# A planned kernel gets new landing times, new GpSimd costs and newly fitted offsets

## The chip, the cores and the metric

The kernel runs on one core of a Trainium2 chip. It is one program of some 108,000 instructions on TensorE (PE), VectorE (DVE), ScalarE (ACT), GpSimd (POOL) and SyncE (SP, which only issues DMAs). The metric is the device time of one execution in microseconds (us).

## The reference

Three stages follow each other on 24576 rows of 256 numbers (8 batches of 3072 rows). All data are float32.

```python
# 1. attention without softmax, z: 64 columns
attn = np.maximum(np.matmul(z, z.transpose(0, 2, 1)) / S, 0.0) ** 2
x = (u * np.matmul(attn, v)).reshape(B * S, D)
# 2. one of 8 experts for each row whose skip score is positive (hidden width 1024)
h = np.maximum(xc[mask] @ w1[e], 0.0)
y[mask] = gate_w[mask, None] * (h @ w2[e])
out[do_compute] = xc + y
# 3. a dense layer with a rational function (hidden width 2048)
h = x @ w_in
P = a[0] + a[1] * h + a[2] * h2 + a[3] * h3
Q = 1.0 + np.abs(b[0]) * np.abs(h) + np.abs(b[1]) * h2
return (P / (Q + 1e-06)) @ w_out
```

## The kernel before

Every float32 operand of a large product is kept as two parts, a rounded one and the rest (names with h and l: `ah`/`al`, `mgh`/`mgl`, the two halves of V, W and mx), and each product is three matmuls.

**Attention** is cut into 1152 ticks. A tick makes 128x512 scores S (L683, L684, 0.467 in the planner's numbers) in a PSUM bank, ScalarE applies Relu (L687), Square (L690) and copies the result to `ah` (L428; sometimes VectorE does, L430), VectorE writes `al` (L698), and PE multiplies both with V (L706). Twelve ticks make a row of 256 outputs; the last one is followed by L766 (`xs`, the product with u, which empties the accumulator), by transposes of `xs` (L782) and by the routing, a chain of small operations (numbered r0 to r24) that ends in indirect DMAs from GpSimd's queue.

**Experts** are units of 256 rows by 256 hidden columns: first layer h (L1133), `mgh` by ScalarE (L1326), `mgl` by VectorE (L1329), second layer (L1152). There are seven groups of 32. For six of them PE runs little else meanwhile. I call these stretches the expert stages; they are those with a high DMA rate. The weights W of each unit (1 MB) are loaded anew for each.

**The dense layer** has 768 units: h (L1144), then a chain on three engines: `mu` = |h| and `mp` by ScalarE (L1334, L1335), q0 = `mq` (L1341 on GpSimd or VectorE, L1339 on ScalarE), q1 and later `gl` by L424 (on either VectorE or GpSimd), logarithm and exponential by ScalarE, and L1347, L1348, L1361, L1362, L1364 on VectorE, then the second layer (L1162). 616 of these units are interleaved with attention ticks. The last 152, at the end of the program, have no attention beside them and use a slightly different chain (L1351 to L1357).

**What sets the order.** Nothing is scheduled by hand. `Flow.add` collects some 14,000 steps, each with a wished time, the steps it comes after, the ring buffers it takes and frees, and a text of costs. `Flow.run` places them one after the other in a model of the queues, and the order in which it places them is the order of the program on each engine. In a cost text such as `"G1.038 Q2.9 L3.3"` a letter is an engine (P TensorE, A ScalarE, D VectorE, G GpSimd, Q the DMA queue), the number is how long the step holds it, a bar separates alternatives of which the planner picks one, and `L` adds time that holds no engine before the result counts as there. Behind an engine's last cost comes `LAT` (2.0 for Q). A final `s` marks a VectorE step and a final `t` a GpSimd step that exclude each other: an `s` step is put off while a `t` step runs, and any GpSimd step while an `s` or `t` step of VectorE runs. The wished time of a step is its place in a regular pattern plus an offset from `PAR`, one for each kind of step and kind of stretch (S, t, a for attention; m, n, x, y for units; `.s` is the program's start). Rings are buffers taken in turn: 5 PSUM banks `b` for scores, h and transposes, 2 `ah`, 2 `al`, 3 each of `mu`, `mq`, `mgh`, `mgl`, 4 `wr` for raw loads of z and V, 8 W, 12 V.

`spacers` are unused columns put ahead of the first tile of a name, which shift the SBUF addresses of what is allocated after it.

## Time and profile before

| | |
|---|---|
| Median of 3 runs | 5405.6 us (5404.68 to 5406.18) |
| The profiled execution, its own time | 5410.29 us |
| its span, first to last instruction | 5408.6 us |
| TensorE busy | 5245.5 us (97%) |
| VectorE busy | 4504.9 us (83%) |
| ScalarE busy | 4193.2 us (78%) |
| GpSimd busy | 3326.9 us (62%) |
| mean granted TensorE clock | 0.997 |

A busy time is the union of an engine's instructions. TensorE's matmuls overlap each other and their ends are modelled, so the pace of a run of matmuls is read from many in a row. In a row of waits stand the engine and line that stood idle, what ended the wait, and then us in total, how many times, and the longest. In a row of the timeline the numbers are start and duration in us; a bracket at the end is the idle time of the engine just before it and what ended it. In a row of groups, the count is followed by busy us, mean ns of one, and the idle time before them with what ended it.

### The profile page before, as it was taken

The page shows a single profiled execution, that of the slowest core. Times are in us where ns is not written, and L with a number is a line of the kernel's source. Part 1 is how long each engine was busy: PE and PEld are TensorE (multiplying, and loading weights), DVE is VectorE, ACT ScalarE, POOL GpSimd, SP SyncE. Part 2 cuts the span into 40 slices and gives each one's busy share as a digit, 9 for nine tenths or more (in the row PEclk, how much of TensorE's full clock was granted, in tenths as well). Part 3 has the DMA queues.
Part 4 walks back from the last instruction along what each step waited for, and adds up shares of the span by engine and source line. Part 5 has one row for each costly group of instructions (what it writes and reads, how often), then busy time and mean ns, then how long its engine had stood idle before and what let it go on. Part 6 is the DMA issues. An engine that isn't in the chain of part 4 may idle for free.

```text
span 5408.6 us, 107807 instructions
## 1 busy us (share of the span) xinstructions
PE 5245.5 (97%) x39885; PEld 4985.3 (92%) x39885; DVE 4504.9 (83%) x7338; ACT 4193.2 (78%) x7643; POOL 3326.9 (62%) x4822
## 2 busy tenths in 40 slices
PE   8999999999999999999999999999999999999988
PEld 8999999999999999899999998999989998889777
DVE  6774789857999958999949999859999589987999
ACT  8885788857888857788848787758888578876998
POOL 5863466635656646557636566536576466666998
PEclk9999999999999999999999999999999999999999
DMA  6747311064100173000372001361011630035000
GB/s 214 251 146 293 105 53 34 30 244 147 52 26 28 56 282 105 24 25 29 106 268 68 27 29 53 137 233 44 25 51 45 242 114 23 28 115 192 22 16 14
DMA packets 218093, 540.19 MB, mean 100 GB/s; under 512 B 30607, under 2 KB 129534, under 8 KB 180946
## 3 DMA queue, kind: packets, MB, share of 16 engines
q1 hardware_dynamic: 188754, 448.71, 23.7%
q0 software_dynamic: 28800, 84.48, 4.5%
q8 instruction: 316, 5.18, 0.4%
q14 instruction: 223, 1.83, 0.1%
HBM read 413.38 MB, written 149.01 MB: 104 GB/s over the span
## 4 chain that ended last, share of the span: by engine, by line
PE 61%; DVE 20%; ACT 6%; POOL 5%; issue 5%; DMA 1%; SPq 0%; DVEq 0%; POOLq 0%; ACTq 0%
PE accA L706 20%; PE h L1144 11%; PE accM L1162 10%; PE h L1133 6%; PE accM L1152 5%; PE S L683 3%; PE S L684 3%; DVE mq L1362 3%; DVE mp L1347 2%; DVE mgh L1361 2%; DVE al L698 2%; DVE h L1348 2%; DVE mq L424 2%; DVE mq L1364 2%; POOL mq L424 1%
## 5 line engine op out<-in xcount | busy, mean ns | idle before, releaser
L706 PE MATMUL accA<-V,ah 128*128 128x256 f32 x9216 | 1271.2, 281 | 21.5 <-ACT ah L428 11.7
L1144 PE MATMUL h<-mx,W 128*128 128x512 f32 x4608 | 1212.8, 399 | 42.0 <-DVE mgl L1357 28.0
L706 PEld LDWEIGHTS accA<-V,ah 128*128 128x128 f32 x9216 | 1161.7, 189 | 36.8 <-ACT ah L428 16.5
L1144 PEld LDWEIGHTS h<-mx,W 128*128 128x128 f32 x4608 | 816.1, 189 | 193.7 <-DVE mgl L1357 37.1
L698 DVE TENSOR_TENSOR al<-S,ah 128x512 fp32r<-128x512 f32 x1152 | 785.1, 683 | 199.6 <-ACT ah L428 185.4
L424 POOL TENSOR_TENSOR mgl<-mq,mu 128x512 fp32r<-128x512 f32 x486 | 641.1, 1319 | 380.4 <-DVE mq L1364 244.5
L1162 PE MATMUL accM<-W,mgh 128*128 128x256 f32 x6144 | 841.6, 280 | 8.3 <-ACT mo L1225 5.9
L687 ACT ACTIVATE S<-S 128x512 f32<-128x512 f32 x1152 | 677.1, 590 | 174.8 <-PE S L684 163.8
L1162 PEld LDWEIGHTS accM<-W,mgh 128*128 128x128 f32 x6144 | 776.0, 189 | 16.5 <-ACT mo L1225 7.5
L1341 POOL TENSOR_SCALAR mq<-mu,coef 128x512 f32<-128x512 f32 x584 | 489.7, 839 | 490.1 <-ACT mu L1334 486.6
L706 PE MATMUL accA<-V,al 128*128 128x256 f32 x4608 | 734.0, 282 | 19.9 <-DVE al L698 19.0
L690 ACT ACTIVATE S<-S 128x512 f32<-128x512 f32 x1152 | 671.4, 585 | 25.5
L706 PEld LDWEIGHTS accA<-V,al 128*128 128x128 f32 x4608 | 623.8, 189 | 32.6 <-DVE al L698 27.3
L1334 ACT ACTIVATE mu<-h 128x512 f32<-128x512 f32 x768 | 455.8, 593 | 237.2 <-PE h L1144 221.7
L424 POOL TENSOR_TENSOR mq<-mq,mu 128x512 f32<-128x512 f32 x458 | 606.5, 1326 | 41.6 <-DVE mq L1341 11.3
L1347 DVE TENSOR_TENSOR mp<-mp,h 128x512 f32<-128x512 f32 x768 | 520.7, 679 | 105.2 <-ACT mp L1335 100.0
L428 ACT ACTIVATE ah<-S 128x512 fp32r<-128x512 f32 x958 | 573.2, 598 | 39.3 <-PE accA L706 11.0
L1335 ACT ACTIVATE mp<-h,coef 128x512 f32<-128x512 f32 x768 | 595.1, 775 | 3.0 <-DVE h L1348 2.8
L684 PE MATMUL S<-T,T 128*128 128x256 f32 x2304 | 589.8, 280 | 1.0 <-ACT T L627 0.9
L1348 DVE SCALAR_TENSOR_TENSOR h<-mp,coef,h 128x512 f32<-128x512 f32 x768 | 572.6, 746 | 4.3
L1362 DVE SCALAR_TENSOR_TENSOR mq<-mq,mgh 128x512 f32<-128x512 f32 x616 | 515.1, 836 | 20.5 <-DVE mgh L1361 0.5
L1359 ACT ACTIVATE mu<-mq 128x512 f32<-128x512 f32 x616 | 388.2, 630 | 179.6 <-DVE mq L424 100.8
(271 smaller groups left out, 9828.3 us busy)
## 6 DMA issues: line engine op xcount, KB each, us to landing
W<-wsc SPq DMA_DIRECT2D x184, 1024.0 KB, 6.8
W<-wsc POOLq DMA_DIRECT2D x48, 1024.0 KB, 5.3
Wv<-wsc SPq DMA_DIRECT2D x64, 512.0 KB, 5.4
xs<-in_u_dram SPq DMA_DIRECT2D x96, 256.0 KB, 3.2
vr<-in_v_dram SPq DMA_DIRECT2D x96, 256.0 KB, 3.1
x<-xs SPq DMA_DIRECT2D x96, 256.0 KB, 2.1
wsc<-wp SPq DMA_DIRECT2D x24, 1024.0 KB, 4.8
mr<-x SPq DMA_DIRECT2D x96, 256.0 KB, 3.4
```

The lines of the kernel that those rows point to most:

```text
L424: (nc.vector if e == "D" else nc.gpsimd).tensor_tensor(*a, **k)
L684: mm(o, lhsT=lw, rhs=T4[b, ic], start=False, stop=(jj == 1), skip_group_check=True)
L687: act(st["s"], st["s"], AF.Relu, scale=1.0 / S)
L690: act(st["s"], st["s"], AF.Square)
L698: ttt(st["lo"], st["s"], st["hi"].bitcast(F32), op=ALU.subtract)
L706: mm(accs[b, ic][:, it * TT : (it + 1) * TT], lhsT=a[:, jj * TT + it * P : jj * TT + (it + 1) * P], rhs=VV[b, jp][:, vi, jj * D : (jj + 1) ...
L1144: mm(h, lhsT=lw, rhs=rw, start=(k == 0 and i == 0), stop=(k == NK - 1 and i == 2), skip_group_check=True)
L1162: mm(accs_[it // 2][:, it % 2 * TT : (it % 2 + 1) * TT], lhsT=(gh, gl)[part][:, it * P : (it + 1) * P], rhs=w[i][:, 512 + ff * D : 512 + ( ...
L1335: pt("p1", "A.664", ["l1b"], lambda: act(buf("mp"), s["h"], AF.Identity, scale=a3, bias=a2), ["mp"])
L1347: pt("p2", "D.602", ["p1", "abs"], lambda: ttt(s["p"], s["p"], s["h"], op=ALU.mult))
L1348: pt("p3", "D.663", ["p2", "abs"], lambda: stt(s["h"], s["p"], a1, s["h"], op0=ALU.add, op1=ALU.mult), (), ["mp"])
L1362: pt("v", "D.602s", ["gh"], lambda: stt(s["q"], s["q"], CQ, s["gh"].bitcast(F32), op0=ALU.add, op1=ALU.mult))
```

## The change

Four things change; the formulas, the steps and the rings do not.

Every load and store gets an `L` with its landing time, or a larger one. Two GpSimd operations that had no mark get a `t`: the copies of 128x512 (`G.588`) and q0 (`G.78`). The load of dense weights by GpSimd's queue costs it 0.52 and not 1.038. All offsets of `PAR` have new values, and with them the order of the whole program. The spacers are three others.

```diff
-    "S.a": 10.7, "S.t": -2.83, "T1.a": -193.43, ... "T1ld.s": -299.17, ... "Vld.s": -133.16, ... "wpld.w": 4.47,
+    "S.a": 11.86, "S.t": -2.87, "T1.a": -92.99, ... "T1ld.s": -330.92, ... "Vld.s": -43.77, ... "wpld.w": -48.08,
...
-    spacers = {"T4": 16, "ah": 16, "W": 112, "mgh": 16}
+    spacers = {"T4": 16, "V": 16, "W": 48}
...
-        add(X(y), k + ("ld",), "Q.36", load, takes=[("wr", k + ("r",)), ("wr", k)])
+        add(X(y), k + ("ld",), "Q.36 L2.8", load, takes=[("wr", k + ("r",)), ("wr", k)])
...
-        add(X(y), k + ("ld",), "Q.73", load, takes=[("wr", k)])
-        add(X(yh), k + ("hi",), "G.588|A.52|D.335s", hi, after=[k + ("ld",)], takes=[("V", k)])
+        add(X(y), k + ("ld",), "Q.73 L2.5", load, takes=[("wr", k)])
+        add(X(yh), k + ("hi",), "G.588t|A.52|D.335s", hi, after=[k + ("ld",)], takes=[("V", k)])
...
-        add(xx, ("u", row), "Q.73", load, takes=[("xs", row)])
+        add(xx, ("u", row), "Q.73 L2.5", load, takes=[("xs", row)])
...
-            (18, 18, "G1.038 L2.4", lambda: r16(2), (16,), [], [], []),
-            (19, 19, "G1.038 L2.4", lambda: r16(3), (16, 17, 18, 21), [], [], [("xs", row)]),
+            (18, 18, "G1.038 L4", lambda: r16(2), (16,), [], [], []),
+            (19, 19, "G1.038 L4", lambda: r16(3), (16, 17, 18, 21), [], [], [("xs", row)]),
...
-            w_first[n][0] - 24.0, ("W", n), "Q1.46 Q1.46" if v else "Q2.9", load, after=dep,
+            w_first[n][0] - 24.0, ("W", n), "Q1.46 Q1.46 L2.2" if v else "Q2.9 L3.3", load, after=dep,
...
-        add(xx, ("W", n), "G1.038 Q2.9", load, after=[("wsc", fp)], takes=[("W", n)])
+        add(xx, ("W", n), "G.52 Q2.9 L.5", load, after=[("wsc", fp)], takes=[("W", n)])
...
-        add(y - 12.0, k + ("ld",), "Q.73 L1.6", load, after=dep, takes=[("mr", (mi, h))])
+        add(y - 12.0, k + ("ld",), "Q.73 L4.9" if m.kind == 1 else "Q.73 L2.6", load, after=dep, takes=[("mr", (mi, h))])
...
-                xe + 2.6, k + ("p1",), "G1.038 L3.4", lambda: scatter(1), after=[k + ("s0",)],
+                xe + 2.6, k + ("p1",), "G1.038 L5", lambda: scatter(1), after=[k + ("s0",)],
...
-            pt("q0", "G.78|A.707|D.46s", ["abs"], q0, ["mq"])
+            pt("q0", "G.78t|A.707|D.46s", ["abs"], q0, ["mq"])
```

The expert weights' first loads and the stores of split weights (`Wl`, `wsc1`, `wsc`) and the stores of results get an `L` in the same way.

Three places in the order of the program show what the offsets do. The numbers in the names count objects (the first) and tiles (the last); `h752` is the first layer of unit 752.

TensorE, an interleaved stretch near the end, from the last score matmul of tick 1099 on. Before:

```order
L684 MATMUL S1099_63513<-T4_7_7_62829,T1_7_3_56503 128x256
L1144 MATMUL h752_63523<-mx83_62894,W232_61272 128x512 x6
L706 MATMUL accA7_7_63093<-V7_6_56951,ah1098_63527 128x256 x8
L706 MATMUL accA7_7_63093<-V7_6_56951,al1098_63534 128x256 x4
L1162 MATMUL accM82_0_62705<-W238_62057,mgh749_63462 128x256 x4
```

and with the change:

```order
L684 MATMUL S1099_63446<-T4_7_7_62821,T1_7_3_56524 128x256
L1144 MATMUL h751_63454<-mx82_62207,W239_62144 128x512 x6
L1162 MATMUL accM82_0_62746<-W237_61873,mgh747_63285 128x256 x4
L1162 MATMUL accM82_1_62747<-W237_61873,mgh747_63285 128x256 x4
L1162 MATMUL accM82_0_62746<-W237_61873,mgl747_63406 128x256 x2
L1162 MATMUL accM82_1_62747<-W237_61873,mgl747_63406 128x256 x2
L706 MATMUL accA7_7_63100<-V7_5_57075,ah1097_63401 128x256 x8
L706 MATMUL accA7_7_63100<-V7_5_57075,al1097_63411 128x256 x4
```

Behind the scores of tick 1099 the next `ah` and `al` products were those of tick 1098; now they are those of tick 1097.

TensorE, inside an expert stage, units 276 to 278. Before:

```order
L1133 MATMUL h276_29342<-mx33_29305,W100_29029 128x256 x12
L1152 MATMUL accM32_0_29215<-W99_28976,mgh275_29310 128x256 x8
L1133 MATMUL h277_29372<-mx33_29305,W101_29109 128x256 x12
L1152 MATMUL accM32_0_29215<-W99_28976,mgl275_29319 128x256 x4
L1152 MATMUL accM33_0_29393<-W100_29029,mgh276_29366 128x256 x8
L1133 MATMUL h278_29410<-mx33_29305,W102_29181 128x256 x12
L1152 MATMUL accM33_0_29393<-W100_29029,mgl276_29370 128x256 x4
```

and with the change:

```order
L1133 MATMUL h276_29333<-mx33_29136,W100_29005 128x256 x6
L1152 MATMUL accM32_0_29196<-W99_28967,mgh275_29319 128x256 x8
L1133 MATMUL h276_29333<-mx33_29136,W100_29005 128x256 x6
L1152 MATMUL accM32_0_29196<-W99_28967,mgl275_29341 128x256 x4
L1133 MATMUL h277_29374<-mx33_29136,W101_29062 128x256 x6
L1152 MATMUL accM33_0_29384<-W100_29005,mgh276_29372 128x256 x8
L1133 MATMUL h277_29374<-mx33_29136,W101_29062 128x256 x6
L1152 MATMUL accM33_0_29384<-W100_29005,mgl276_29393 128x256 x4
```

Between h276 and the product with `mgh276` stood 24 matmuls of 256 columns; now 10 stand there, since each first layer is cut in two halves with a second layer between them.

SP, the start, from the first load of z on. Before:

```order
L589 DMA zr0_0_124<-in_z_dram 128x256
L589 DMA zr0_1_127<-in_z_dram 128x256
L665 DMA xs0_130<-in_u_dram 128x2x256
L665 DMA xs1_132<-in_u_dram 128x2x256
L1412 DMA xs_71<-dflt_117 16x2064
L639 DMA vr0_0_139<-in_v_dram 128x512
```

With the change the first four rows are the same, then come `wr1_8mu` and:

```order
L383 DMA wr1_8mq_135<-in_moe_w2_dram 128x2x256
L379 DMA wr1_9mu_138<-in_moe_w1_dram 128x2x256
L383 DMA wr1_9mq_139<-in_moe_w2_dram 128x2x256
L1412 DMA xs_71<-dflt_117 16x2064
L379 DMA wr1_10mu_146<-in_moe_w1_dram 128x2x256
L383 DMA wr1_10mq_147<-in_moe_w2_dram 128x2x256
L589 DMA zr0_2_166<-in_z_dram 128x256
L589 DMA zr0_3_176<-in_z_dram 128x256
L1412 DMA xs_71<-dflt_117 16x2064
L1396 DMA ov_73<-ovf_200 1x2
L1412 DMA xs_71<-dflt_117 16x2064 x2
L639 DMA vr0_0_240<-in_v_dram 128x512
```

The first chunk of V, `vr0_0`, was the sixth load from there on and is now the eighteenth. In the same stretch ScalarE's order is Relu of ticks 0 to 3, Square and `ah` of tick 0, Square of tick 1, and only then the copy that reads `zr0_2`; that copy stood behind the Relu of tick 0 before.

## Rows read from the trace of the kernel before

**Rows 1.** The page, first part: busy us, share of the span, instructions.

```profile
PE 5245.5 (97%) x39885; PEld 4985.3 (92%) x39885; DVE 4504.9 (83%) x7338; ACT 4193.2 (78%) x7643; POOL 3326.9 (62%) x4822
```

**Rows 2.** Windows of 135 us: bounds, length, each engine's busy us, clock, DMA.

```profile
1890.00:2025.00 135.00, 131.42 (x1106) 129.41 (x1105) 73.56 (x131) 71.57 (x134) 56.91 (x105) 1.00 0.76 279
...
5130.00:5265.00 135.00, 121.47 (x737) 107.11 (x736) 131.45 (x205) 125.09 (x213) 126.16 (x114) 0.96 0.06 20
...
sum 5400.00, PE 5245.49 PEld 4985.31 DVE 4504.91 ACT 4193.23 POOL 3326.88; mean PE 131.14 PEld 124.63 DVE 112.62 ACT 104.83 POOL 83.17
```

**Rows 3.** Waits of PE: us in total, times, longest.

```profile
PE h L1144 <- DVE mgl L1357: 28.0, 27, 3.2
PE accA L706 <- DVE al L698: 19.0, 27, 2.8
PE tp L605 <- DVE zh L598: 16.7, 6, 10.5
PE accM L1162 <- DVE mgl L1357: 13.1, 12, 2.3
PE accA L706 <- ACT ah L428: 11.7, 18, 1.5
...
PE accA L706 <- DVE xs L766: 7.0, 9, 1.7
...
PE xp L782 <- DVE xs L766: 5.7, 9, 1.5
```

**Rows 4.** Timeline around 4511 us, three engines.

```profile
4503.88 1.28 POOL L424 TENSOR_TENSOR mq<-mq,mu 128x512 f32<-128x512 f32 x1
...
4504.15 1.60 DVE L1362 SCALAR_TENSOR_TENSOR mq<-mq,mgh 128x512 f32<-128x512 f32 x1
...
4510.37 0.68 DVE L698 TENSOR_TENSOR al<-S,ah 128x512 fp32r<-128x512 f32 x1
...
4511.11 0.74 PE L706 MATMUL accA<-V,al 128*128 128x256 f32 x4 [1.38 <-DVE al L698]
```

**Rows 5.** Chain that ended last, one piece: start, us, what.

```profile
147.53 2.83 PE accA L706 x24
```

**Rows 6.** Groups by line: count, busy us, mean ns, idle before.

```profile
L698 DVE TENSOR_TENSOR al<-S,ah 128x512 fp32r<-128x512 f32 x1152 | 785.1, 683 | 199.6 <-ACT ah L428 185.4 <-PE accA L706 3.3 <-PE S L684 3.2
...
L1341 POOL TENSOR_SCALAR mq<-mu,coef 128x512 f32<-128x512 f32 x584 | 489.7, 839 | 490.1 <-ACT mu L1334 486.6 <-DVE al L698 1.3
...
L1362 DVE SCALAR_TENSOR_TENSOR mq<-mq,mgh 128x512 f32<-128x512 f32 x616 | 515.1, 836 | 20.5 <-DVE mgh L1361 0.5 <-POOL rin L760 0.5
...
L424 DVE TENSOR_TENSOR mq<-mq,mu 128x512 f32<-128x512 f32 x310 | 279.2, 901 | 3.3 <-POOL mq L1341 3.1
...
L1152 PE MATMUL accM<-W,mgh 128*128 128x256 f32 x1536 | 210.9, 280 | 0.0
```

**Rows 7.** DMA issues: count, KB each, median us from issue to landing.

```profile
vr<-in_v_dram SPq DMA_DIRECT2D x96, 256.0 KB, 3.1
...
mr<-xs SPq DMA_DIRECT2D x56, 258.0 KB, 6.3
```

**Rows 8.** Waits of all engines, one row.

```profile
POOL mti L1211 <- DMA mr<-xs: 79.3, 20, 8.3
```

**Rows 9.** Timeline of the start, four engines.

```profile
10.43 0.35 SPq L639 DMA_DIRECT2D vr<-in_v_dram  x1
...
14.02 0.62 POOL L432 TENSOR_SCALAR V<-vr 128x512 fp32r<-128x512 f32 x1 [7.23 <-DMA vr<-in_v_dram]
...
17.71 0.60 ACT L428 ACTIVATE ah<-S 128x512 fp32r<-128x512 f32 x1
...
18.45 1.83 PE L706 MATMUL accA<-V,ah 128*128 128x256 f32 x7 [1.48 <-ACT ah L428]
```

**Rows 10.** Timeline in an expert stage, one unit's first layer and `mgh`.

```profile
2009.19 1.53 PE L1133 MATMUL h<-mx,W 128*128 128x256 f32 x12
...
2010.76 0.60 ACT L1326 ACTIVATE mgh<-h 128x512 fp32r<-128x512 f32 x1 [2.55 <-PE h L1133]
```

More of the change, by code (lines that the diff above doesn't have):

```diff
@@ L1008, in plan_w1 @@
         room = [("l1a", max(0, w_last[n - NW] - 2))] if n >= NW else []
-        add(xx - 5.0, ("Wl", n), "Q.73 Q.73", load, after=room, takes=tr)
-        add(xx, ("Wh", n, 0), "A.52|D.335s|G.588", lambda e: hi(e, 0), after=[("Wl", n)], takes=[("W", n)])
-        add(xx + 0.6, ("Wh", n, 1), "A.52|D.335s|G.588", lambda e: hi(e, 1), after=[("Wh", n, 0)])
+        add(xx - 5.0, ("Wl", n), "Q.73 Q.73 L4.2", load, after=room, takes=tr)
+        add(xx, ("Wh", n, 0), "A.52|D.335s|G.588t", lambda e: hi(e, 0), after=[("Wl", n)], takes=[("W", n)])
+        add(xx + 0.6, ("Wh", n, 1), "A.52|D.335s|G.588t", lambda e: hi(e, 1), after=[("Wh", n, 0)])
         add(xx + 0.8, ("Wo", n), "D.602s|G1.245t", lambda e: lo(e, 0), after=[("Wh", n, 0)], frees=tr[:1])
         add(xx + 1.4, ("W", n), "D.602s|G1.245t", lambda e: lo(e, 1), after=[("Wh", n, 1), ("Wo", n)], frees=tr[1:])
-        add(xx + 2.0, ("wsc1", c), "Q2.9", store, after=[("W", n)])
+        add(xx + 2.0, ("wsc1", c), "Q2.9 L1", store, after=[("W", n)])
     def plan_w1prep(c, y):
@@ L1036, in store @@
             nc.sync.dma_start(out=wsc1[c].bitcast(F32), in_=st["w"].bitcast(F32))
-        add(X(y), k + ("ld",), "Q.73 Q.73", load, takes=tr)
+        add(X(y), k + ("ld",), "Q.73 Q.73 L2.7", load, takes=tr)
         for half in range(2):
             h = k + (half,)
-            add(X(y + 2.0 + 0.3 * half), h, "G.588|D.335s", lambda e, half=half: hi(e, half), after=[k + (("ld",) if half == 0 else (0,))], takes=[] if half else [("mx", k)])
+            add(X(y + 2.0 + 0.3 * half), h, "G.588t|D.335s", lambda e, half=half: hi(e, half), after=[k + (("ld",) if half == 0 else (0,))], takes=[] if half else [("mx", k)])
             add(X(y + 2.4 + 0.6 * half), h + ("l",), "G1.245t", lambda e="G", half=half: lo(e, half), after=[h], frees=tr[half : half + 1])
-        add(X(y + 4.0), ("wsc1", c), "Q2.9", store, after=[k + (0, "l"), k + (1, "l")], frees=[("mx", k)])
+        add(X(y + 4.0), ("wsc1", c), "Q2.9 L1", store, after=[k + (0, "l"), k + (1, "l")], frees=[("mx", k)])
     def whole(n):
@@ L1107, in plan_w2prep @@
         k = ("wsc", fp)
-        add(X(y), k + (0,), "Q1.46 Q1.46", load, after=[("wsc", fp - 1)] if fp else [], takes=[("W", k + ("a",)), ("W", k + ("b",))])
+        add(X(y), k + (0,), "Q1.46 Q1.46 L3", load, after=[("wsc", fp - 1)] if fp else [], takes=[("W", k + ("a",)), ("W", k + ("b",))])
         for half in range(2):
@@ L1122, in plan_w2prep @@
             add(X(y), h + ("l",), "D.602s", lambda half=half: lo(half), after=[h + ("h",)], frees=[("wr", h)])
[L1123 removed]
+        add(X(y + 0.7), k, "G1.038 Q2.9 L1", store, after=[k + (1, "l")], frees=[("W", k + ("w",))])
     def mm_l1(h, w, xh, xl, ffs=(0, 1)):
@@ L1272, in plan_half @@
         else:
-            add(xe + 1.0, k + ("p1",), "Q.73", store, after=[k + ("p0",)], frees=[("mo", (mi, h))])
+            add(xe + 1.0, k + ("p1",), "Q.73 L1.5", store, after=[k + ("p0",)], frees=[("mo", (mi, h))])
     def WV(n):
```

25 lines of the change are left out of this document (12 added, 13 removed), and 38 rows, old and new, of the table PAR.

## The prediction

> **What bounds the kernel now.** I read the page's first part, then the table of windows, then the waits of PE, and only then single stretches. TensorE is busy for 5245.5 of 5408.6 us [rows 1]; the 40 windows leave it 154.5 us idle [rows 2]. So nothing that the change does to another engine is worth more than those idle times, and the matmuls themselves are the same 39885 in another order. The windows say where the idle time sits. In the window of the expert stage PE loses 3.6 us of 135. In the last stage it loses 13.5 us, and there VectorE is busy for 131.5 of 135 us: VectorE sets the end of that stage, whatever order PE has. The waits of PE [rows 3] name what ended its idle times: `mgl` (28.0 and 13.1 us, nearly all in the last stage), `al` and `ah` of the attention ticks (19.0 and 11.7), `xs` at the ends of attention rows (7.0 and 5.7), and `zh` (16.7, of which 10.5 is the start of the program). Nothing on this list is a DMA: a late landing reaches PE only through an engine that stands behind it.
>
> Why a tick waits is seen at 4511 us [rows 4]: PE stands 1.38 us for `al`. VectorE was late because L1362, which takes 0.68 us when nothing interferes, took 1.60 us: GpSimd was in a whole-tile product until 4505.16, and L1362 ended 0.59 us after that. Everything behind it on VectorE came later by as much. PE's order left little room: from the scores of that tick to their use it had 7.0 us of other work. I count such room throughout as the matmuls that stand between in PE's order, at 0.118 us per 256 columns (24 in 2.83 us [rows 5]).
>
> **Part 1: PE's places for the attention ticks.** The new numbers draw the uses of `ah` and `al` back. Between a tick's scores and its `al` product PE has 10.8 us of other work in the median where it had 8.8; before its `ah` product 9.4 where it had 7.0. Ticks with under 7 us ahead of `al` fall from 336 to 70 of 1152. The tick of 4511 us goes from 7.0 to 13.0. The waits for `al` and `ah` are 19.0 + 11.7 = 30.7 us [rows 3]. If they go with the number of short ticks, 70/336 = 0.21 of them stay, 6.4 us, and 24 us go. If they stay whole, since `ah` has two buffers and the room from the last use of tick n-2 to the `ah` product of tick n is 5.5 us where it was 5.1, nothing goes. The row of 4511 us is nearer to the first end: `al` was late there by VectorE's queue, not by a missing buffer. I take **-16 us**, range -24 to 0. What is late next is the S bank (five in the ring): its room stays at 8.3 us, before 8.4, so I add nothing for that.
>
> **Part 2: ends of attention rows.** The first `ah` product of a row waits for L766 to empty the accumulator. From row 17 on, 24 of 79 row ends had less than 1.5 us of PE work there; now 7 have. Of 7.0 us [rows 3], 17/24 is 5. The transposes of `xs` (5.7 us) have a median of 1.4 us ahead of them where they had 1.9, so nothing is gained on them. I take **-4**, range -5 to 0.
>
> **Part 3: what the planner knows of GpSimd, and who does what.** L1362 and L424 on VectorE read two SBUF tiles. L698, of the same size but with one operand in PSUM, means 0.683 us; L1362 means 0.836 (616 times) and L424 0.901 (310 times) [rows 6]. The excess is 616 x 0.153 + 310 x 0.218 = 162 us of VectorE. It comes from GpSimd's whole-tile operations; the planner already held VectorE back for its products, and not for L1341, which ran 584 times for 489.7 us. A third of the excess, 54 us, is the most I give to L1341. VectorE also gets 25 instructions fewer (39 `ah` go to ScalarE, 21 q0 leave VectorE; V, q1 and gl come back), 25 x 0.68 = 17 us, and ScalarE 50 more, 30 us, which its 78% hide [rows 1]. Of 54 + 17 us on an engine with 83% only the stretches count in which PE waits for VectorE; I take **-6**, range -15 to 0. A reason against more: the row of 4511 us also shows the products, which the planner did know, blocking L1362. [...]
>
> **Part 4: landing times.** The planner took 0.73 + 2.0 = 2.73 us for a load of `vr`; the trace says 3.1, so it came late as a rule. It takes 5.23 now. For `mr` out of `xs` it took 4.33 against 6.3, and takes 7.63 now [rows 7]. GpSimd lost 79.3 us to late `mr` [rows 8], in a stage where it has slack: its 62% hide that. On PE's path I find only the `zh` waits outside the start, 16.7 - 10.5 = 6.2 us. I take **-3**, range -6 to 0. A longer assumed landing also holds ring buffers longer in the plan; that is priced in the next part, where it bites.
>
> **Part 5: the start.** SP's queue is moved as a whole: six loads of `wr1_8` to `wr1_10` and two more `z` chunks go ahead of the first `vr`. That has two consequences. SP needs about 0.5 us for each issue. And `vr0_0` is now the ninth taker of the four `wr` buffers and waits for `zr0_2` to be read by VectorE, whose ScalarE step stands behind the scores' first steps: ScalarE writes `ah` of tick 0 from 17.71 us [rows 9]; its steps start some 0.5 us apart, one more stands ahead of `zh0_2`, so that starts at 18.7, and VectorE is done with it near 19.8. Before, `vr0_0` went out at 10.43 and GpSimd had it at 14.02, 3.6 us later; then 0.62 us on GpSimd and about 0.68 on VectorE for the two halves. So the first product stands at 19.9 + 3.6 + 1.3 = 24.8 us, where it stood at 18.45. PE does 0.9 us of later work ahead of it. The loss is up to 5.4 us; V chunks follow at the pace of the ring, so I expect little of it back. **+5**, range 0 to +8. ScalarE, GpSimd and SP have nothing else urgent queued there.
>
> **Part 6: the expert stage.** Here the change takes room away. In 192 units (six stages of 32) PE had a median 3.3 us of work between h and the `mgh` product, and 5.6 us to the `mgl` product; now 1.2 and 2.8. ScalarE writes `mgh` in 0.60 us, starting 0.04 us after the matmuls' end in the row [rows 10]; counted from PE's next free slot this is about 0.85 us, so 0.3 us of slack is left. Queued on ScalarE between two `mgh` stand `mx`, and now and then a copy of V, which waits for a landing. Before, PE had next to nothing to wait for there, so no gain is possible. Bounds: 0, and 192 x 0.2 = 38 us if a unit waits 0.2 us on average. I take **+3**, nearer to the first: some twenty units of before had 0.9 us of room too, and the group of all 1536 `mgh` products shows 0.0 us of idle time ahead of them [rows 6]. `W` slots come free some 2.8 us sooner, which helps the loads of that stage.
>
> **Part 7: no price.** The last stage is VectorE's. Its three windows leave VectorE 3.5 us idle in the one shown, about 9 in all, so it can gain 9 at the most; I take 0, range -9 to +6. The spacers keep what a matmul reads together 64 bytes apart (modulo 128), as before; I take 0 for them.
>
> **The sum.** -16 - 4 - 6 - 3 + 5 + 3 = -21 us. The profiled run took 5410.3 us, 4.7 above the median of 5405.6; 5389 against the first is 5385 against the second. **Forecast: 5385 us.**
>
> **The rivals.**
> First, **slower: the expert stage has no slack left.** If ScalarE reaches `mgh` late, by a V copy that waits for its load or by an `mx`, each unit's wait falls straight on PE. At 0.2 us per unit it costs 38 us instead of 3: 5385 + 35 = 5420. It outweighs the gains from (21 + 3)/192 = 0.125 us per unit on. For it: the room fell by more than half in the stage with the most DMA. Against: ScalarE is busy only 71.6 of 135 us there [rows 2]. Chance 0.24, with all other ways to lose as much.
> Second, **no change: room is not what ticks lack.** The buffers of `ah` and VectorE's queue, both as full as before, set the waits; parts 1 and 3 come to 0 and the time is 5385 + 16 + 6 = 5407. This is also the case in which new landing times change numbers of a plan and not the chip. Chance 0.21.
> Third, **the block only changes hands**: kept off VectorE's back, L1341 waits for VectorE instead (it means 0.84 us now [rows 6]) and what follows on GpSimd comes later; part 3 is 0, the time 5391. Chance 0.15.
> The forecast itself has 0.40.
>
> **How the numbers follow.** A measurement of this kernel tells about 0.2%, 11 us, from no change: 5395 and 5416 are the edges. The forecast and the third rival are faster (0.55), the second the same (0.21), the first slower (0.24). The terms' own ends give 5405.6 - 24 - 5 - 15 - 6 - 9 = 5347 below; above, the slower rival at 5420 must be half inside. Range 5350 to 5424.
>
> **What would show it right or wrong.** Part 1: waits of PE for `al` and `ah` near 15 us in sum, not 31. Part 3: L1362 near 0.80 us in the mean. Part 4: the wait of GpSimd for `mr` well under 79 us. Part 5: the first accA matmul at 23 to 25 us. Part 6: in the windows of the expert stages PE as busy as before (131 to 135 us) and no wait of PE for `mgh`; a row "PE accM <- ACT mgh L1326" of 20 us or more means the first rival. If PE's idle total falls and the time does not, the count of room was the wrong measure.

## The result, and the profile after

The changed kernel takes 5465.9 us in the median of four runs (5455.98 to 5466.58) where the kernel before took 5405.9 beside it: ratio 1.0105, 95% interval 1.0088 to 1.0123. It is slower by 60 us by the medians, 57 by the ratio; 5385 was forecast, and 5424 was the upper end of the range. The profiled execution of after is its fastest run, 5455.98 us with a span of 5454.3; it is compared with the span of 5408.6 before, so the two profiles hold 45.7 us of the difference.

The first part of the page of after, beside [rows 1]:

```profile
PE 5296.4 (97%) x39885; PEld 5020.7 (92%) x39885; DVE 4508.2 (83%) x7313; ACT 4198.2 (77%) x7693; POOL 3282.6 (60%) x4797
```

PE's idle time is 5454.3 - 5296.4 = 157.9 us, before 163.1. So PE's idle time did not grow: PE is **busy** 50.9 us longer, with the same 39885 matmuls. The prediction summed idle times only, since "the matmuls themselves are the same 39885 in another order".

The waits of PE after (total us, times, longest), beside [rows 3]:

```profile
PE accM L1162 <- DVE mgl L1357: 49.4, 37, 5.1
PE tp L605 <- DVE zh L598: 14.6, 4, 10.4
PE xp L782 <- DVE xs L766: 14.4, 21, 2.5
PE h L1144 <- DVE mq L1364: 10.8, 21, 1.5
...
PE accA L706 <- DVE xs L766: 4.1, 6, 1.3
...
PE accA L706 <- DVE al L698: 3.1, 5, 1.5
...
PE accA L706 <- ACT ah L428: 2.0, 3, 1.6
```

The waits for `al` and `ah` fell from 30.7 to 5.1 us, as Part 1 wanted and more. Others took their place: `mgl` of the last stage (28.0 + 13.1 before, 49.4 + 0.7 now), `xs` ahead of its transposes (5.7, now 14.4).

Where the busy time comes from is seen in the chain that ended last, taken in windows of 100 us (start, us, what). First a piece of after that answers to [rows 5], then one of the kernel **before** that the prediction's rows do not have:

```profile
58.08 2.83 PE accA L706 x24
```

```profile
711.80 2.72 PE accA L706 x24
```

The same 24 products take 2.83 us or 2.72 us, 117.9 or 113.3 ns each, though nothing interrupts either piece. Of the pieces of this kind in before's chain, 9 of 24 took 2.72 and 10 took 2.83 us. In after's chain none of 59 took less than 2.82, and 50 took 2.83. So a product of 256 columns has two paces here, and the changed kernel has lost the better one.

For the whole program I used the start times of all products. Where the next one starts within 1.15 times 118 ns (256 columns) or 1.15 times 233.5 ns (512 columns), I take it that nothing held it, and the distance is its pace. Where the distance is longer, what is over 118 or 233.5 ns counts as a wait. By this count after's products run 49.3 us slower than before's and its waits are 4.2 us shorter. The sum, 45.1, is nearly the difference of the two spans, 45.7. **In this account the loss lies in the pace of products that wait for nothing.** It is an account and not yet a cause: slower products also leave the other engines more time, and so hide waits. The experiments below part the two.

Rows of after that answer to [rows 2], [rows 6] and [rows 7]: one window, groups by line, DMA issues.

```profile
1890.00:2025.00 135.00, 134.91 (x1105) 132.28 (x1104) 87.93 (x152) 84.79 (x158) 61.03 (x101) 1.00 0.62 222
```

```profile
L1362 DVE SCALAR_TENSOR_TENSOR mq<-mq,mgh 128x512 f32<-128x512 f32 x616 | 527.3, 857 | 17.5
...
L1341 POOL TENSOR_SCALAR mq<-mu,coef 128x512 f32<-128x512 f32 x598 | 495.6, 829 | 674.2 <-ACT mu L1334 655.4 <-DVE al L698 8.7 <-DVE mq L1364 6.1
```

```profile
vr<-in_v_dram SPq DMA_DIRECT2D x96, 256.0 KB, 3.6
...
mr<-xs SPq DMA_DIRECT2D x56, 258.0 KB, 6.8
```

The window from 1890 us does not hold the same work in both: the expert stage in it begins at 1925 us before and at 1949 us after (312 and 210 of the stage's first-layer matmuls start in the window). So here are the six expert stages themselves, each from its first to its last first-layer matmul, as the sum of six windows, before and then after:

```profile
sum 674.00, PE 669.99 PEld 668.10 DVE 257.48 ACT 259.35 POOL 207.88; mean PE 111.66 PEld 111.35 DVE 42.91 ACT 43.22 POOL 34.65
```

```profile
sum 697.00, PE 696.30 PEld 694.48 DVE 268.26 ACT 278.52 POOL 216.38; mean PE 116.05 PEld 115.75 DVE 44.71 ACT 46.42 POOL 36.06
```

PE has next to no idle time there, before or after. The lengths are not to be compared: matmuls of other kinds run among those of the stages, and the six windows hold 5764 in all before and 5953 after.

### The profile page after: what moved, and what is told of

Its sections match the earlier page's. It is cut to its first block, busy times and chain, and to the rows that moved or that the text cites. A ratio compares the mean times of both kernels' runs of the same rounds, so it can differ in the third digit from the quotient of the medians.

```text
span 5454.3 us, 108022 instructions
## 1 busy us (share of the span) xinstructions
PE 5296.4 (97%) x39885; PEld 5020.7 (92%) x39885; DVE 4508.2 (83%) x7313; ACT 4198.2 (77%) x7693; POOL 3282.6 (60%) x4797
## 4 chain that ended last, share of the span: by engine, by line
PE 68%; DVE 17%; ACT 7%; issue 5%; POOL 4%; DMA 1%; DVEq 0%; SPq 0%; POOLq 0%; ACTq 0%
PE accA L706 22%; PE h L1144 12%; PE accM L1162 12%; PE h L1133 6%; PE accM L1152 6%; PE S L683 4%; PE S L684 4%; DVE mq L1362 3%; DVE mp L1347 2%; DVE mq L424 2%; DVE mgh L1361 2%; DVE al L698 2%; DVE mq L1364 1%; DVE h L1348 1%; ACT mp L1335 1%
## 5 line engine op out<-in xcount | busy, mean ns | idle before, releaser
L706 PEld LDWEIGHTS accA<-V,ah 128*128 128x128 f32 x9216 | 1179.1, 188 | 30.2 <-ACT ah L428 4.0
L698 DVE TENSOR_TENSOR al<-S,ah 128x512 fp32r<-128x512 f32 x1152 | 785.8, 683 | 238.1 <-ACT ah L428 212.3
L1144 PEld LDWEIGHTS h<-mx,W 128*128 128x128 f32 x4608 | 814.0, 189 | 168.9 <-DVE mq L1364 15.3
L1341 POOL TENSOR_SCALAR mq<-mu,coef 128x512 f32<-128x512 f32 x598 | 495.6, 829 | 674.2 <-ACT mu L1334 655.4
L1162 PE MATMUL accM<-W,mgh 128*128 128x256 f32 x6144 | 855.3, 281 | 2.4 <-DVE mgh L1354 2.0
L1162 PEld LDWEIGHTS accM<-W,mgh 128*128 128x128 f32 x6144 | 791.9, 189 | 17.6 <-DVE mgh L1354 2.5
L428 ACT ACTIVATE ah<-S 128x512 fp32r<-128x512 f32 x997 | 596.5, 599 | 60.6 <-PE accA L706 46.2
L1162 PE MATMUL accM<-W,mgl 128*128 128x256 f32 x3072 | 499.5, 284 | 52.8 <-DVE mgl L1357 49.4
L1362 DVE SCALAR_TENSOR_TENSOR mq<-mq,mgh 128x512 f32<-128x512 f32 x616 | 527.3, 857 | 17.5
```

Source lines behind the costliest of these rows:

```text
L698: ttt(st["lo"], st["s"], st["hi"].bitcast(F32), op=ALU.subtract)
L706: mm(accs[b, ic][:, it * TT : (it + 1) * TT], lhsT=a[:, jj * TT + it * P : jj * TT + (it + 1) * P], rhs=VV[b, jp][:, vi, jj * D : (jj + 1) ...
L1144: mm(h, lhsT=lw, rhs=rw, start=(k == 0 and i == 0), stop=(k == NK - 1 and i == 2), skip_group_check=True)
L1162: mm(accs_[it // 2][:, it % 2 * TT : (it % 2 + 1) * TT], lhsT=(gh, gl)[part][:, it * P : (it + 1) * P], rhs=w[i][:, 512 + ff * D : 512 + ( ...
L1362: pt("v", "D.602s", ["gh"], lambda: stt(s["q"], s["q"], CQ, s["gh"].bitcast(F32), op0=ALU.add, op1=ALU.mult))
```

## The experiments: the addresses

What could slow a product that waits for nothing? The changed kernel computes the same from other SBUF addresses. Each product has two operands: a block of 128x128, which a row of its own loads (PEld) and which I call the weights, and the moving operand of 256 or 512 columns. In the trace the load for the **next** product lies inside the running one (in before for 33352 of the 34303 products that start less than 130 ns after the one ahead). So what may meet is one product's moving operand and the next one's weights. For the products of V the moving operand is `V` and the weights are `ah` or `al`; for the second layers the moving operand is `W` and the weights are `mgh` or `mgl`. In both kernels the spacers put these 64 bytes apart modulo 128; but before, `ah` stands 64 bytes past `V` modulo 256, and after 192 bytes past it, and `mgh` to `W` likewise. (The other candidate, TensorE's clock, does not fit: its mean is 0.997 before and 0.995 after, and the two pieces above both lie where it is at its upper level: 1.00 from 58 to 61 us in after, and from 711 to 715 us in before.)

**Both kernels, flipped by 64 bytes.** My first theory was the class modulo 128: before, the moving operand stands at 96 and the weights at 32, after the other way about.

```diff
-    spacers = {"T4": 16, "V": 16, "W": 48}
+    spacers = {"T4": 16, "mx": 16, "V": 16, "W": 48}
```

> The changed kernel with one more spacer of 64 bytes ahead of mx. Every instruction, wait and place is that of the changed kernel; only the SBUF addresses of mx, ah, al, V, W, mgh and mgl move by 64 bytes, so that modulo 128 each stands where it stood in the kernel before. Theory 'addresses' (matmuls that wait for nothing run at a pace that depends on where their operands lie; about 50 us of the changed kernel's busy PE are that): near 5410, in any case under 5425, PE busy near 5245 us, and 256-column products of V near 116.3 ns from start to start instead of 117.7. Rival 'order' (the pace comes from the new order, its waits or the clock): 5456 to 5466 as the changed kernel itself, products of V near 117.7 ns.

```diff
-    spacers = {"T4": 16, "ah": 16, "W": 112, "mgh": 16}
+    spacers = {"T4": 16, "V": 16, "ah": 16, "W": 112, "mgh": 16}
```

> The kernel before with one more spacer of 64 bytes ahead of V, so that V, W, ah, al, mgh, mgl and mx stand modulo 128 where the changed kernel has them; no instruction moves. Theory 'addresses': 5445 to 5465, products of V near 117.7 ns from start to start (before: 116.3). Rival 'order': 5406 as before, 116.3 ns.

Measured: 5466.3 us, ratio to before 1.0107 (1.0090 to 1.0123), and 5401.9, ratio 0.9985 (0.9976 to 0.9995). The class modulo 128 is out: neither kernel took the other's time, and the second even gained. Since a flip of everything keeps the differences modulo 256, that difference was left as a candidate.

**The pace by itself.** Beside these two ran a program of products alone:

> A program of its own that leaves out the whole computation: 240 blocks of 24 products of 256 columns, whose moving operand and weights stand at 0, 32, 64 or 96 bytes modulo 128 in all 16 combinations, five blocks each, first alone, then beside work of ScalarE and VectorE, then beside loads. Two products of other widths stand ahead of each block. Theory 'addresses': the mean from start to start differs between the combinations, (32, 96) near 117.7 ns and (96, 32) lower, some near 113.3. Rival 'order': all combinations agree within 0.5 ns, and if two paces are seen they go by the stretch, not by the address.

Each combination had its own mean, the same within 0.2 ns alone, beside ScalarE and VectorE, and beside loads (the first block of the program apart): 113.4 to 114.0 ns for (96, 32), 117.8 for (32, 96), 118.2 to 120 where both have the same class. So here the address does set the pace, and these other engines do not. The tiles stood there at 128 and 0 modulo 256, so (96, 32) is a difference of 64 and (32, 96) one of 192: the same sides as in the two kernels. The second program went through all differences:

> A program of its own that leaves out the whole computation: blocks of 16 products of 256 columns (six blocks for each pair of addresses) and of 8 products of 512 columns (three), whose moving operand and weights stand at 0 to 224 bytes modulo 256 in all 64 combinations; three products of other widths ahead of each block. Theory 'difference modulo 256': the mean depends on weights minus moving operand modulo 256, not on either alone: 64 often near 113.5 ns, 192 near 117.7, 0 and 128 near 118.7, 32 near 119.8. Rival: the differences 64 and 192 have the same mean over the blocks, and only what stands ahead of a block sets its pace.

Eight neighbouring blocks of it, moving operand at 128 and weights at 0, 32, ... 224, as pieces of the chain (start, us; L42 is the block of 16, L36 the products of other widths):

```profile
368.51 1.93 PE acc L42 x16
...
370.76 1.93 PE acc L42 x16
...
373.02 1.90 PE acc L42 x16
...
375.24 1.88 PE acc L42 x16
...
377.44 1.92 PE acc L42 x16
...
379.69 1.91 PE acc L42 x16
...
381.93 1.84 PE acc L42 x16
...
384.09 1.90 PE acc L42 x16
```

The seventh, weights 64 past the moving operand, is the short one. All blocks, mean ns from start to start:

| weights minus moving, modulo 256 | 0 | 32 | 64 | 96 | 128 | 160 | 192 | 224 |
|---|---|---|---|---|---|---|---|---|
| 256 columns (47 or 48 blocks each) | 119.7 | 118.2 | 115.0 | 118.2 | 119.0 | 120.0 | 117.1 | 117.1 |
| blocks under 115 ns | 0 | 0 | 30 | 0 | 0 | 0 | 8 | 0 |
| 512 columns (24 blocks each) | 228.9 | 233.1 | 233.3 | 234.0 | 233.2 | 233.6 | 230.1 | 233.1 |

At 64 and 192 a block runs near 113.3 (up to 114.9) or at 117.8 and stays there; which, goes with what stood ahead of it. At 64 it is mostly the first, at 192 mostly the second. Both theories had a part right. Two things stay open. Inside a block a product's own weights and the next one's have the same address modulo 256, so the program can't tell which of the two meets the moving operand. And why the difference matters at all, no run shows.

**The two kernels, with that difference alone exchanged.**

```diff
-    spacers = {"T4": 16, "V": 16, "W": 48}
+    spacers = {"T4": 16, "V": 48, "W": 48, "mgh": 32}
```

> The changed kernel with V and W 128 bytes further and mgh 256 bytes further; no instruction moves. Theory 'difference modulo 256' (formed after both kernels with a flip of 64 bytes kept their time): a product runs at 113.3 or at 117.7 ns per 256 columns, and it finds the faster pace when its next weights lie 64 bytes past its moving operand modulo 256, and hardly ever when they lie 192 bytes past it. The changed kernel has ah - V = 192 and mgh - W = 192, the kernel before 64 and 64; this one has 64 and 64. Expected 5385 to 5415, products of V and ah near 116 ns or below in the mean (5456 to 5466 and 117.7 in the changed kernel). Rival 'order' (the new order of the products sets the pace, addresses don't): 5456 to 5466, 117.7 ns.

```diff
-    spacers = {"T4": 16, "ah": 16, "W": 112, "mgh": 16}
+    spacers = {"T4": 16, "ah": 48, "W": 16, "mgh": 48}
```

> The kernel before with ah, al, mgh, mgl and mx moved by 128 bytes against V and W, so that ah - V and mgh - W are 192 modulo 256 as in the changed kernel; no instruction moves. Theory 'difference modulo 256': 5440 to 5465, products of V and ah near 117.7 ns. Rival 'order': 5400 to 5410, near 116 ns as before.

Measured: the changed kernel comes down to 5434.4 us, ratio 1.0041 (1.0027 to 1.0055); the kernel before goes up to 5442.4, ratio 1.0060 (1.0043 to 1.0077). The second is as the theory said. The first gained 31 us (35 by the ratios) but stayed 19 us above the upper end of what was expected. For each kernel the first part of the page and one piece of its chain; the changed kernel at 64:

```profile
PE 5243.5 (97%) x39885; PEld 4972.7 (92%) x39885; DVE 4515.3 (83%) x7313; ACT 4194.8 (77%) x7693; POOL 3288.8 (61%) x4797
```

```profile
56.29 2.73 PE accA L706 x24
```

The kernel before at 192:

```profile
PE 5290.8 (97%) x39885; PEld 5022.5 (92%) x39885; DVE 4517.9 (83%) x7338; ACT 4196.7 (77%) x7643; POOL 3334.7 (61%) x4822
```

```profile
146.53 2.83 PE accA L706 x24
```

PE's busy time has changed sides, 5243.5 and 5290.8, without an instruction having moved. All kernels in one table, each against the kernel before; products and waits counted as above from the profiled run:

| kernel | `ah` - `V` mod 256 | products of V under 115 ns | products, us | waits, us | span, us | ratio of times |
|---|---|---|---|---|---|---|
| before | 64 | 38% | 0 | 0 | 0 | 1 |
| after | 192 | 3% | +49.3 | -4.2 | +45.7 | 1.0105 |
| e1_after_flip | 192 | 4% | +48.3 | +3.0 | +52.6 | 1.0107 |
| e2_before_flip | 64 | 56% | -20.2 | +6.9 | -12.7 | 0.9985 |
| e3_after_64 | 64 | 68% | -23.2 | +46.6 | +21.7 | 1.0041 |
| e4_before_192 | 192 | 8% | +46.2 | -16.7 | +30.2 | 1.0060 |
| e7_after_as_before | 64 | 41% | 0.0 | +31.2 | +29.8 | 1.0050 |
| f1_before_best | 64 | 70% | -29.2 | +19.5 | -9.3 | 0.9979 |

Read e3 against after: products 72.5 us faster, waits 50.8 us longer, 24 us of span won. My reading is that faster products reach their inputs earlier while the other engines are no faster; about 10 of the 50.8 us are products at the lower clock (see the next section; the mean granted clock is 0.993 in e3, 0.995 in after).

**A better place for the kernel before.**

```diff
-    spacers = {"T4": 16, "ah": 16, "W": 112, "mgh": 16}
+    spacers = {"T4": 48, "ah": 16, "W": 48, "mgh": 16}
```

> The kernel before with T4, V, ah and W moved by 128 bytes against T1, and W's spacer cut by 256 bytes; no instruction moves. The differences ah - V and mgh - W stay 64 modulo 256; those at the seams become 64 too: T1 - T4 (was 192), T1 - V and T1 - W (192), with ah - T4 64 as before. Theory 'difference modulo 256': the scores' products find the faster pace more often (mean 117.4 before) and hand it on to the products of V behind them; 5375 to 5398. Rival 'seams don't matter': 5403 to 5412.

Measured: 5400.9 us, ratio 0.9979 (0.9970 to 0.9989). With e2_before_flip it is the fastest kernel here, 3 us above what was expected. The products of V gained (70% at the better pace). The scores did not: those at a seam, the place where one pair of operands follows another, mean 119.3 ns with a difference of 64, and had 117.8 with 192 before. So what holds inside the blocks does not hold for them. 19.5 of 29.2 us came back as waits.

## The experiments: the plan

**At equal addresses.** What is the plan worth when every address difference is the one of before?

```diff
-    spacers = {"T4": 16, "V": 16, "W": 48}
+    spacers = {"T4": 16, "mx": 16, "V": 48, "W": 48, "mgh": 32}
```

> The changed kernel with spacers that give it every address difference modulo 256 that the kernel before has (of ah, al, V, mgh, mgl, W, mx, T1 and T4 against each other); no instruction moves. What is left between it and the kernel before is the plan: the order of the work, who does what, and the waits. Theory 'two causes': the addresses were some 31 to 33 of the 56 us and the plan is the rest, so 5425 to 5440. Rival 'addresses alone': 5395 to 5412, the plan neutral or better. Products of V and ah near 115 to 116 ns in both.

Measured: 5439.9 us, ratio 1.0050 (1.0034 to 1.0067). The theory of two causes holds: about 27 us are the plan's (18 to 36 by the interval). The products run as before (0.0 us), so by the count the whole difference is waits, +31.2 us. This is the clean test of Parts 1 to 6, which gave -21. Waits of PE in e7_after_as_before, as above:

```profile
PE accM L1162 <- DVE mgl L1357: 53.8, 36, 5.1
PE xp L782 <- DVE xs L766: 16.5, 21, 2.6
...
PE h L1144 <- DVE mq L1364: 12.3, 21, 1.6
...
PE h L1144 <- DVE al L698: 9.3, 18, 1.4
PE t4p L624 <- DVE al L698: 5.0, 7, 1.6
...
PE accA L706 <- DVE al L698: 2.9, 4, 1.5
PE accA L706 <- ACT ah L428: 2.6, 4, 1.5
```

Idle rows miss waits under some 0.16 us, since a product is shown busy for 280 ns while the next starts 118 ns after it. So here is the count from start to start, by what PE waits ahead of (us). The rows hold waits behind products of 256 and 512 columns; the last row adds all others.

| ahead of | before | e7 | e8_old_room | e9_xp_later | g3_after_old_last |
|---|---|---|---|---|---|
| products of V | 74.0 | 38.0 | 118.1 | 59.7 | 41.2 |
| first products of the x units (`h`) | 26.1 | 46.1 | 30.5 | 40.7 | 42.2 |
| transposes of `xs` (`xp`) | 7.0 | 22.6 | 19.8 | 6.9 | 22.8 |
| scores | 23.0 | 28.9 | 29.1 | 45.4 | 27.9 |
| `t4p` | 4.7 | 11.2 | 0.1 | 13.0 | 11.8 |
| last stage's products | 76.2 | 83.0 | 79.4 | 82.5 | 80.5 |
| all waits, against before | 0 | +31.2 | +71.7 | +67.1 | +20.2 |

The room of Part 1 is there and gives 36 us. The x units' `h`, `xp`, the scores and `t4p` give 48 back: they wait for VectorE's `mq` (L1364) and `al`, which free their PSUM banks, and for `xs`.

**Not all of these are waits.** In stretches where the granted clock is at its lower level (0.50 from 1349.4 to 1352.6 us in before) products start 213 ns apart for 256 columns and 427 ns for 512, and the count puts down what is over 118 and 233.5 ns as a wait. One such stretch of e7, where PE had stood idle for 5.10 us (clock 0.83 in the mean of the window):

```profile
5000.00:5020.00 20.00, 14.04 (x82) 12.62 (x83) 19.40 (x31) 15.17 (x25) 15.19 (x14) 0.83 0.21 66
```

Past the first 35 us, where the records of the clock begin at different places, e7 has the lower level for 60 us in all, before for 34, g3_after_old_last for 39. Products that start at the lower level's distance make up 20.3 us of e7's waits, 10.5 of before's and 11.9 of g3_after_old_last's. So some 10 of the 31.2 us are products at the lower clock, 8 of them in the last stage, and some 21 are waits. How much of the span these 10 us cost was not tried by itself.

**The old room.** Is the room at fault?

```diff
-    "avh.t": 3.49,
-    "avl.t": 0.57,
+    "avh.t": 0.2,
+    "avl.t": -2.0,
```

> As e7_after_as_before, with two offsets of the attention ticks drawn forward (avh.t 0.2 for 3.49, avl.t -2.0 for 0.57), so that PE has again what it had before between a tick's scores and its uses: 6.95 us of work to ah and 8.4 to al in the median, 260 ticks under 7 us (kernel before: 6.95, 8.8 and 336; e7: 9.4, 10.8 and 70). Counted as time from start to start over 118 ns per 256 columns, e7 waits 38 us ahead of the products of V (before: 74) and 109 us ahead of the transposes of xs, the x units' first products, t4p and the scores (before: 61). Theory 'the waits change hands': products of V back to 60 to 80, the other four down by 20 or more, the whole at 5428 to 5450. Rival 'room is a plain gain, something else loses': products of V up by 30 and the other four as in e7, 5460 to 5475. Rival 'these offsets are the loss': 5410 to 5425.

Measured: 5484.2 us, ratio 1.0145 (1.0128 to 1.0162), slower than all three cases had it. The room is not the loss: without it the products of V wait for 118 us. That waits change hands is there in its direction, since the other four fall from 108.8 to 79.5; but it isn't a zero sum.

**The row ends.** The transposes of `xs` placed later:

```diff
-            (0, 0, "D.602", r0, (),
+            (0, 0, "D.602 L1", r0, (),
```

> As e7_after_as_before, and the planner takes VectorE's step at a row's end (L766) to land 1 us later, so that PE's transposes of xs stand later in its order. e7 waits 22.6 us ahead of them (before: 7.0). Theory 'PE comes too early to the row ends': the wait falls under 10 us and the whole by 8 to 15 us, to 5425 to 5432. Rival 'handed on': the wait falls and others grow by as much, 5434 to 5446.

Measured: 5476.5 us, ratio 1.0129 (1.0112 to 1.0146), slower than both cases had it. The wait went as aimed, 22.6 to 6.9 us, and other waits grew by 51.6: the scores by 16, the products of V by 22.

**The costs alone**, in the kernel before, with its offsets and its address differences:

```diff
-    spacers = {"T4": 16, "ah": 16, "W": 112, "mgh": 16}
+    spacers = {"T4": 16, "ah": 16, "V": 48, "al": 16, "W": 48, "mgh": 16}
-        add(X(y), k + ("ld",), "Q.73", load, takes=[("wr", k)])
+        add(X(y), k + ("ld",), "Q.73 L2.5", load, takes=[("wr", k)])
...
```

> The kernel before, its offsets kept, with all the new costs: landing times and the marks on GpSimd's operations; spacers set so that every address difference modulo 256 is that of the kernel before. Theory 'the costs are worth little by themselves, the offsets moved the waits': within 12 us of the kernel before on either side, 5398 to 5422. Rival 'the costs are the gain': 5380 to 5395. Rival 'a plan holds only for the costs it was fitted to': over 5430.

Measured: 5524.0 us, ratio 1.0201 (1.0184 to 1.0219), as the last rival had it: these offsets hold only with the costs they were fitted to.

**How much is a step beside the fit worth at all?** Two numbers moved by a hair, in each kernel:

```diff
-    "avl.t": 1.4,
-    "l1a.x": 3.96,
+    "avl.t": 1.5,
+    "l1a.x": 3.9,
```

> The kernel before with two offsets moved by a hair: avl.t 1.5 for 1.4 and l1a.x 3.9 for 3.96, in the planner's microseconds; address differences as before. The planner puts thousands of instructions elsewhere all the same. Theory 'a fitted plan is a narrow place' (what the partial steps lost beside e7 is the price of leaving the fit, so they price no single part): 5420 to 5450. Rival 'the plan is smooth' (such a step costs little, so the losses of the partial steps belong to what each changed): 5402 to 5416.

```diff
-    "avl.t": 0.57,
-    "l1a.x": 4.84,
+    "avl.t": 0.67,
+    "l1a.x": 4.78,
```

> As e7_after_as_before with two offsets moved by a hair: avl.t 0.67 for 0.57 and l1a.x 4.78 for 4.84. Theory 'a fitted plan is a narrow place': 5450 to 5480. Rival 'the plan is smooth': 5432 to 5448.

Measured: 5422.2 us, ratio 1.0018 (1.0008 to 1.0027), and 5458.2, ratio 1.0089 (1.0072 to 1.0106): +9 us on the kernel before and +18 on e7. The second is where the theory of a narrow place had it; the first is at that theory's lower edge, and by its ratio, 0.18%, under it. So even a step that means nothing cost 9 and 18 us (10 and 21 by the ratios), in one try each. The losses of the three partial steps, 37 to 111 us, are more than that, but terms of 3 to 16 us, as mine were, can't be told from it one by one.

**The last stage.** First its 17 unit offsets, then all 38 that bear on it, put back in e7:

```diff
-    "l1a.y": 13.46, "l2h.y": 12.66,
+    "l1a.y": 7.14, "l2h.y": 3.6,
...
```

> As e7_after_as_before, and the 17 offsets of the last stage's units (the keys that end in .y) with the numbers of the kernel before; addresses as there. Theory 'the last stage loses': between the 152nd and the last of the last stage's first products the changed kernel takes 430.4 us and the kernel before 418.8, whatever the addresses (433.2 and 419.9 or 417.9), because PE stands for mgl with the next unit's first product behind it; with the old numbers it takes 416 to 423, and the whole comes 8 to 16 us under e7. Rival 'no place of its own': the stage is VectorE's in any order, its loss comes from when it can start, and the whole stays within 4 us of e7.

```diff
-    "l1a.n": 17, "l2h.n": 20.5,
+    "l1a.n": 13.02, "l2h.n": 15.07,
...
```

> As e7_after_as_before with all 38 offsets of the last stage and of the expert units that run beside its first part (keys that end in .y, .n, .2y and .1n) as in the kernel before. e7 loses 12.6 us on the kernel before between the 152nd and the last of the last stage's first products. Theory 'the last stage's own offsets lose it': that stretch back to 416 to 423 us from 431.4, no later a start into it, the whole 5424 to 5432. Rival 'it is what the stretch inherits' (as when the 17 offsets of the units alone were put back, which gave 423.5 and a start 9 us later): 5434 to 5446.

Measured: 5436.0 us, ratio 1.0042 (1.0025 to 1.0059), and 5433.0, ratio 1.0043 (1.0026 to 1.0060). The stretch that is compared runs from the 152nd to the last of the 912 first-layer matmuls of this stage, which is the last 127 of its 152 units. With the unit offsets alone it took 423.5 us but began 9 us later, so nothing was won. With all 38 it took 419.3 us and began 1.5 us later, and PE's sum of waits fell by 11.0 us. So the stretch went as the theory had it. The whole did not clearly: the gain on e7 is 7 us by the medians and 4 by the ratios, whose intervals overlap, and the median lies between the theory's upper end, 5432, and its rival's lower one, 5434. The stretch in one window each: before, e7, and e7 with all 38 put back.

```profile
4964.50:5383.30 418.80, 378.34 (x2317) 332.04 (x2316) 409.36 (x638) 394.96 (x670) 399.70 (x361) 0.98 0.06 20
```

```profile
4983.10:5414.50 431.40, 381.98 (x2326) 330.85 (x2324) 415.17 (x642) 396.79 (x667) 401.00 (x364) 0.97 0.06 20
```

```profile
4984.60:5403.90 419.30, 375.13 (x2298) 327.99 (x2297) 407.95 (x635) 393.72 (x667) 399.16 (x362) 0.99 0.06 20
```

VectorE is idle there for 9.4 us, 16.2 and 11.3, and busy for 409.4, 415.2 and 408.0. How that comes about shows in e7's timeline (start, us, engine, line, tiles; in brackets the idle time and what ended it):

```profile
4997.28 3.37 DVE L1341 TENSOR_SCALAR mq<-mu,coef 128x512 f32<-128x512 f32 x1
...
4997.82 1.31 POOL L1355 TENSOR_TENSOR mq<-mq,mgh 128x512 f32<-128x512 f32 x1
...
4999.08 1.27 POOL L424 TENSOR_TENSOR mq<-mq,mu 128x512 f32<-128x512 f32 x1
...
5003.74 0.68 DVE L1357 TENSOR_TENSOR mgl<-h,mu 128x512 fp32r<-128x512 f32 x1
...
5004.47 1.23 PE L1162 MATMUL accM<-W,mgl 128*128 128x256 f32 x4 [5.10 <-DVE mgl L1357]
...
5005.49 2.76 PE L1144 MATMUL h<-mx,W 128*128 128x512 f32 x6
...
5008.29 0.60 ACT L1334 ACTIVATE mu<-h 128x512 f32<-128x512 f32 x1 [1.22 <-PE h L1144]
...
5008.99 0.77 POOL L1341 TENSOR_SCALAR mq<-mu,coef 128x512 f32<-128x512 f32 x1 [0.54 <-ACT mu L1334]
```

It begins with one instruction of VectorE, q0 (L1341). It takes 0.54 us in the median of this run, and here it took 3.37: it ended 0.30 us after two whole-tile products that GpSimd ran one behind the other. In the same stretch of the kernel before, the longest q0 on VectorE took 1.04 us; with all 38 offsets back VectorE has none there. PE then stands 5.10 us for `mgl`, and the next unit's first product, which needs nothing of it, stands behind in PE's order. Until it has run, ScalarE and GpSimd, and behind them VectorE, lack a unit. And that first product (six of 512 columns in 2.76 us, elsewhere 1.55) runs at the lower clock. In the whole stage products at the lower clock take 15.3 us more than at the upper one in e7, 7.5 before and 5.1 with the 38 offsets back.

## Why the prediction was wrong, point by point

- **Part 7, the spacers, is the step that failed first.** "The spacers keep what a matmul reads together 64 bytes apart (modulo 128), as before; I take 0 for them." Modulo 256 they went from 64 to 192. That is 46 us of slower products and 32 us of time in the old plan (e4 against before), and 49 and 30 us in the new one (after against e7). What led to it is the premise that the matmuls are the same, and the pace of 0.118 us "(24 in 2.83 us)", which is one of two that stand in the same view of before.
- **Part 1** named the right mechanism and sized it low: the waits for `al` and `ah` fell by 25.6 us, taken were 16. But "what is late next" was looked for in the S bank alone, "so I add nothing". The banks of `h` and `t4p`, the scores and `xp` gave back 48 us by the count from start to start.
- **Part 2**: the waits for `xs` ahead of the products fell by 2.9 of the 4 taken; ahead of the transposes, where the room went from 1.9 to 1.4 us and I took nothing, they rose by 8.7.
- **Part 3** was wrong. L1362 means 0.857 us, not near 0.80 (0.836 before): fewer of them were held up (123 over 0.9 us, before 143), but for longer (1.50 us in the mean of these, before 1.30). What holds them up is seen in before: the 350 that ran beside no 128x512 operation of GpSimd took 0.686 us in the mean and 0.764 at most, the other 266 took 1.035; L698 took 0.683 without one and 0.682 beside one. The block stays on VectorE: L1341 on GpSimd is as short as before (829 ns, before 839), so it didn't change hands either, as the third rival had it.
- **Part 4** was wrong in the sign it named: GpSimd waits 113.0 us for `mr` (79.3 before), and the loads themselves landed later (`vr` 3.6 us, before 3.1; `mr` 6.8, before 6.3). PE's waits for `zh` fell by 2.1 of the 3 us taken.
- **Part 5** was right. The first product of V stands at 23.79 us, forecast 23 to 25, and 72 ticks on e7 is 4.1 us behind the kernel before, taken were 5. The rows of after beside [rows 9]:

```profile
19.96 0.37 SPq L639 DMA_DIRECT2D vr<-in_v_dram  x1
...
23.12 0.62 POOL L432 TENSOR_SCALAR V<-vr 128x512 fp32r<-128x512 f32 x1 [7.30 <-DMA vr<-in_v_dram]
...
23.79 2.59 PE L706 MATMUL accA<-V,ah 128*128 128x256 f32 x8 [1.07 <-POOL V L432]
```

- **Part 6** was right, and the first rival is out: no wait of PE for `mgh` of the expert stage is among its rows, and PE is busy for 696.3 of the 697 us of the six stages. The result is on this rival's side, slower, by other mechanisms.
- **Part 7, the last stage**: 0 taken, range -9 to +6; e7 loses 12.6 us between the 152nd and the last of its first products, and the 38 old offsets give that back in the stretch.
- The last sentence of the prediction held: PE's idle total fell and the time did not, so the count of room was the wrong measure, for the pace it was counted in.

In sum, some 57 us by the ratios. The four combinations of plan and address difference:

| ratio to the kernel before | difference 64 | difference 192 |
|---|---|---|
| old plan | 1 | 1.0060 (e4) |
| new plan | 1.0050 (e7) | 1.0105 (after) |

The addresses are worth 30 to 32 us and the new plan 24 to 27, each known to some 9 us. Of the plan's share 4 us are the start and 4 to 10 the last stage's offsets. The other 13 to 19 us are spread over the rest, waits and some products at the lower clock, and no partial step showed a single cause of them; that stays open.

## What to carry to other kernels

Where PE is busy for 97% of the span, compare how long the same row of products takes in several places before you count idle times: two paces in one kernel are a reason to suspect the addresses, and here three spacers moved about as much time as a new order of the whole program. A change that moves allocation is to be timed once with the old address differences, so that the layout and the plan are priced apart. In a fitted order like this one, a wait that was removed came back where PE reached the next thing earlier: sum the waits by what stands behind them, not only at the place you mend. And set products at a lower granted clock apart before you call their time a wait.
